# Two memory-attention layers and two gated layers on one core: a stored order for the engines, and zero matmuls in TensorE's planned waits

## The chip, the cores and the metric

The kernel runs on one core of one Trainium2 chip. The metric is the device time of that core in microseconds (us). Before the change it is 1828.59 us, the median of three runs (1826.58 to 1828.89). A change of under about 0.2% (3.7 us) can't be told from none.

The engines are named as in the profile: PE (TensorE, matmuls), PEld (its weight loads), DVE (VectorE), ACT (ScalarE), POOL (GpSimd) and SP (SyncE, which here only issues transfers).

## The reference, cut to what matters

```
def _A_ref(x, mem0, Wq, Wk, Wv, Wo, seg_len):          # x [1, 2048, 512], 32 heads of 128, seg_len 32
    mask = (idx[:, None] < 8) | (idx[:, None] >= idx[None, :])
    mem = mem0                                         # 8 rows
    for s in range(64):
        h = concatenate([mem, x[:, 32 * s:32 * s + 32]])              # 40 rows
        q, k, v = h @ Wq, h @ Wk, h @ Wv                              # per head
        p = softmax(where(mask, q @ k.T * scale, -1e9))
        o = (p @ v) @ Wo                                              # summed over heads
        mem = o[:, :8]                                 # carried to the next segment
        outs.append(o[:, 8:])

def _B_ref(x, w_gate, w_up, w_down):                   # 512 -> 1792 -> 512
    return (sigmoid(x @ w_gate) * (x @ w_up)) @ w_down

x = x + _A_ref(layernorm(x), ...)
x = x + _B_ref(layernorm(x), ...)
x = x + _A_ref(layernorm(x), ...)                      # the same weights again
x = x + _B_ref(layernorm(x), ...)
```

The 64 segments of one attention layer are a chain, for each one needs the memory rows that the segment before it made.

## The kernel before, in words

**Tiling and staging.** The four attention weights stay in SBUF. The two attention layers run side by side: layer 0 works on segment t while layer 1 works on segment t - 6, so there are 70 steps. In the middle 58 steps both layers share their matmuls, which then have 80 moving columns (40 rows of each layer); in the first 6 and the last 6 steps there is one layer and 40 columns. The lines below are those of the kernel before.

One step (`emit_step`) goes through six groups of up to six heads. For each group: Q and K (task `qk`, L734, 8 matmuls a head), a copy of the PSUM bank to `qku` on ACT, scores (`sc`, L748), mask, maximum, subtraction, exponential, sum and scaling on DVE and ACT (L762 to L779), transposes of the probabilities (`ptr`, L791), copies to `ptsb` (ACT or DVE), the product with V (`pvm`, L814), a copy to `otsb` on ACT, and the output projection (`wom`, L832), which gathers all heads in one PSUM bank. At the end of the step DVE copies the memory rows (L845, L850) into the `hT` tile of the next step, and only then can the next step's Q and K start. V of the 24 or so rows of x is made ahead in passes of 128 rows (`vmm`, L583), sent to a scratch tensor and fetched again; V of the memory rows is made in "strips" (L660).

The gated layer (`ffn`) works on blocks of 128 rows, one block of each layer for every four steps: transposes (L900, L552), gate and up (L932), tanh on ACT, the product on DVE, and the down projection (L956). Its weights don't fit and are fetched again for every block: POOL issues the transfers of `wg`, `wu` and `wd` into rings of three tiles each (L924, L925, L950).

**What sets the order.** No engine reorders whole tasks on the chip; the program's text fixes each engine's order. The kernel first records its work as 13,300 tasks with dependences (`Planner.add`), each with a modelled duration. `Planner.forward` then plays the tasks through a model of the five engines: whenever an engine is free, it takes the ready task with the greatest `tail`, if a buffer is free for it. In the kernel before, `tail` comes at first from the longest way to the end, and is then set anew 23 times by `backward`, which plays the plan in reverse; the order with the shortest modelled span is kept. The instructions are emitted in the order of the modelled start times. Every task has a latency to its reader (`LAT`, `TO_PE`, and `late` for single tasks).

Of the kernel before, what the change touches and what calls it, by code (L numbers as in the profile page):

```python
# [2 lines left out]

# [6 lines left out]
BF16 = mybir.dt.bfloat16  # L10
# [6 lines left out]
P = 128  # L17
MEM = 8
SEG = 32
L = MEM + SEG  # L20
# [11 lines left out]
def mm_ns(n):  # L32
    return max(n / 2.4 + 2.3, 26.0)

# [12 lines left out]


class Task:
    __slots__ = ("eng", "dur", "lat", "fn", "deps", "succ", "tail", "boost", "ndep", "ready", "start", "idx", "on", "fresh", "acq", "rel", "durs", "tick", "prev", "land", "adj", "banks")  # L50

    def __init__(self, eng, dur, lat, fn, boost):
        self.durs = dur if isinstance(dur, dict) else {e: dur for e in eng}
        self.eng, self.dur, self.lat, self.fn, self.boost = eng, min(self.durs.values()), lat, fn, boost
        self.deps, self.succ, self.fresh = set(), [], set()
        self.acq, self.rel = [], []
        self.on = None
        self.land = 3000.0
        self.adj = {}
        self.banks = ()  # L60


# [19 lines left out]
class Planner:  # L82
# [4 lines left out]
    TO_PE = 32.0  # L87
    WAIT = 65.0

    def __init__(self):  # L90
        self.tasks = []
        self.writer = {}
        self.readers = {}
        self.bufs = []
# [6 lines left out]
    def add(self, eng, dur, fn, r=(), w=(), lat=None, boost=0.0, use=(), late=0.0):  # L101
        engs = eng if isinstance(eng, tuple) else (eng,)
        tk = Task(engs, dur, self.LAT[engs[0]] if lat is None else lat, fn, boost)
        tk.idx = len(self.tasks)
        for k in r:
            if k in self.writer:
                tk.deps.add(self.writer[k])
                tk.fresh.add(self.writer[k])
        for k in w:
            if k in self.writer:  # L110
                tk.deps.add(self.writer[k])
            for q in self.readers.get(k, ()):
                tk.deps.add(q)
        for k in w:
            self.writer[k] = tk.idx
            self.readers[k] = []
        for k in r:
            self.readers.setdefault(k, []).append(tk.idx)
        tk.deps.discard(tk.idx)
        if late:  # L120
            tk.adj = {d: late for d in tk.fresh if self.tasks[d].eng == ("PE",)}
        self.tasks.append(tk)
        if engs[0] != "PE":
            tk.banks = tuple(k for k in r if isinstance(k, Buf) and k.pool.psum)
        for k in list(r) + list(w) + list(use):
            if isinstance(k, Buf) and (not k.users or k.users[-1] != tk.idx):
                k.users.append(tk.idx)
        return tk
# [7 lines left out]

    def plan(self, rounds=24):

        T = self.tasks
# [3 lines left out]
        for bf in self.bufs:  # L143
# [3 lines left out]
            for u in set(bf.users):  # L147
                T[u].rel.append(bf)
        for tk in reversed(T):
            m = 0.0  # L150
            for s in tk.succ:
                m = max(m, T[s].tail + self.gap(tk, T[s]))
            tk.tail = m + tk.dur + tk.boost
        best = None
        self.spans = []
        for k in range(rounds):
            if k:
                self.backward()
            order = self.forward()
            self.spans.append(self.span)  # L160
            if best is None or self.span < best[0]:
                best = (self.span, order, [tk.start for tk in order], [tk.on for tk in order], [bf.slot for bf in self.bufs])
        self.span, order, starts, ons, slots = best
        for tk, st, on in zip(order, starts, ons):
            tk.start, tk.on = st, on
        for bf, sl in zip(self.bufs, slots):
            bf.slot = sl
        return order

    def backward(self):  # L170

        T = self.tasks
        left = [len(tk.succ) for tk in T]
        rdy = [0.0] * len(T)
        free, heaps, events = {}, {}, []
        end = [tk.start + tk.dur for tk in T]
        for tk in T:
            free.setdefault(tk.on, 0.0)
            heaps.setdefault(tk.on, [])
            if left[tk.idx] == 0:  # L180
                heapq.heappush(events, (0.0, tk.idx))
        n, now = len(T), 0.0
        while n:
            while events and events[0][0] <= now:
                i = heapq.heappop(events)[1]
                if i >= 0:
                    heapq.heappush(heaps[T[i].on], (-end[i], i))
            did = False
            for e, h in heaps.items():
                if free[e] > now or not h:  # L190
                    continue
                tk = T[heapq.heappop(h)[1]]
                fin = now + tk.dur
                free[e] = fin
                tk.tail = fin + tk.boost
                heapq.heappush(events, (fin, -1))
                n -= 1
                did = True
                for d in tk.deps:
                    rdy[d] = max(rdy[d], fin + self.gap(T[d], tk))  # L200
                    left[d] -= 1
                    if left[d] == 0:
                        heapq.heappush(events, (rdy[d], d))
            if not did and n:
                now = max(now, events[0][0])

    def forward(self):
# [127 lines left out]
        return order  # L335

    def waits(self, tk, seen):

# [18 lines left out]
class Kern:  # L357
# [40 lines left out]
    def setup_tiles(self):  # L398
# [11 lines left out]
        self.ident, self.maskb, self.mask1 = cst[:, 0:P], cst[:, P:P + L], cst[0:L, P + L:P + 2 * L]  # L410
        self.negh = cst[:, P + 2 * L:P + 2 * L + 2].bitcast(F32)
        small = c.tile([P, 48], F32, name="small")
        self.lns = [small[:, 10 * i:10 * i + 10] for i in range(3)]
# [33 lines left out]
    def setup_consts(self):  # L447
# [8 lines left out]
        nc.gpsimd.affine_select(out=self.maskb[0:L, 0:SEG], in_=self.maskb[0:L, 0:SEG], pattern=[[-1, SEG]],  # L456
                                compare_op=ALU.is_ge, fill=NEG, base=0, channel_multiplier=1)
        nc.vector.memset(self.negh[:], -0.5)

    def clear(self):  # L460
# [11 lines left out]
        for k, t_ in enumerate(self.vsb):  # L472
            pl.add("POOL", 1800, lambda t_=t_: nc.gpsimd.memset(t_[32:64], 0.0),
                   w=[(n, j, k, i) for n in ("vs", "vx") for j in (0, 1) for i in (0, 1)])
# [194 lines left out]
    def emit_step(self, t):  # L669
# [11 lines left out]
        full = slice(0, LW)  # L681
        hkeys = [("hT", slot, j, k) for j in jobs for k in ("m", "x")]

        c0 = 0 if both else L * j0
# [34 lines left out]
        for g, (heads, us) in enumerate(self.groups):  # L719
# [90 lines left out]
            def pvm(us=us, ptsb=ptsb, OB=OB):  # L810
# [11 lines left out]
            pl.add("ACT", act_ns(gsz * ncol, True), lambda hs=hs, gsz=gsz, otsb=otsb, OB=OB: (  # L822
                otsb[:, hs, 0:ncol], OB[:, 0:gsz * ncol].rearrange("p (h q) -> p h q", q=ncol)), r=[OB], w=[("otsb", oi)])

# [27 lines left out]
        for idx, j in enumerate(jobs):  # L852
# [4 lines left out]
            pl.add("ACT", 160, lambda dst=dst, a=48 * j - c0: (dst, wo3(a, SEG)), r=[WB], w=[("oxT", j, oi, s % BLK)])  # L857

    def last_weights(self):

        if self.lw is None:
# [3 lines left out]
            for jp in range(self.FC // 2):  # L865
                row = []
                for nm, ring, n in (("wg", self.wg, self.NG), ("wu", self.wu, self.NG), ("wd", self.wd, self.ND)):
# [3 lines left out]
                    else:  # L871
# [6 lines left out]
                    src = self.wdv[:, 2 * jp:2 * jp + 2, :] if nm == "wd" else (self.wgv if nm == "wg" else self.wuv)[:, :, jp * 2 * P:(jp + 1) * 2 * P]  # L878
                    pl.add("POOL", 760, lambda tl=tl, src=src: nc.gpsimd.dma_start(out=tl[:, :, :], in_=src), w=keys, lat=6000.0,
                           r=[("vs", 1, (2 * (self.NSTEPS - 1) + q) % self.NV, i) for q in range(2) for i in range(2)] if k else [])  # L880
# [4 lines left out]
    def ffn(self, j, b, q0=0, nq=BLK):  # L885
# [15 lines left out]

        pl.add("PE", DC * mm_ns(P), tr, r=[("oxT", j, b % 2, q) for q in range(q0, q0 + nq)], w=[OB])
        si = self.xw[(j, b)]
# [11 lines left out]
        for jp in range(FC // 2):  # L915
# [3 lines left out]
            else:  # L919
# [3 lines left out]
                bt = ["boot"] if self.cnt["wg"] <= self.NG else []  # L923
                pl.add("POOL", 760, lambda wg=wg, fs=fs: nc.gpsimd.dma_start(out=wg[:], in_=self.wgv[:, :, fs]), r=[("wo", self.H - 1)], w=[gk] + bt, lat=6000.0)  # L924
                pl.add("POOL", 760, lambda wu=wu, fs=fs: nc.gpsimd.dma_start(out=wu[:], in_=self.wuv[:, :, fs]), r=[("wo", self.H - 1)], w=[uk] + bt, lat=6000.0)  # L925
            GB = pl.buf(self.bank, "bg")
# [16 lines left out]
        for ip in range(FC // 2):  # L943
# [3 lines left out]
            else:  # L947
                di = self.nxt("wd", self.ND)
                wd, dk = self.wd[di], ("wd", di)
                pl.add("POOL", 760, lambda wd=wd, ip=ip: nc.gpsimd.dma_start(out=wd[:], in_=self.wdv[:, 2 * ip:2 * ip + 2, :]),  # L950
                       w=[dk] + (["boot"] if self.cnt["wd"] <= self.ND else []), lat=6000.0)

# [72 lines left out]
    def run(self):  # L1025
# [4 lines left out]
        with self.tc.manual_schedule():  # L1030
            self.setup_consts()
            for tk in order:
                got = tk.fn()
                if isinstance(got, tuple) and len(got) == 3:
# [64 lines left out]
```

## Time and profile before

| | before |
|---|---|
| time, median of 3 | 1828.59 us |
| span of the profiled run | 1828.3 us |
| PE busy | 1763.5 us |
| DVE busy | 1178.3 us |
| ACT busy | 1175.2 us |
| POOL busy | 580.2 us |
| mean granted clock of PE | 0.994 |
| HBM traffic over the span | 135 GB/s |

How to read it: "busy" counts the time in which an engine has an instruction in work. A matmul's record is longer than the time until the next may start (about 200 ns against 36 ns at 80 columns), so PE can be busy through a short stall. "Idle before" is the time that an engine had nothing in work, and behind the arrow stands what ended it. The chain of waits is followed back from the last instruction. The granted clock is the share of full speed at which PE was let run.

### The profile page before, as it was taken

Reading aid. Unit: us, or ns where it says so; the run is one execution under the profiler, and the core shown is the slowest. Engines: PE = TensorE matmul, PEld = TensorE weight load, DVE = VectorE, ACT = ScalarE, POOL = GpSimd, SP = SyncE. Lnnn points to the kernel's source line nnn. Section 1 sums busy time; section 2 is a strip of 40 time slices with the busy share of each in tenths; the row PEclk is TensorE's granted clock in tenths of the full one; section 3 lists DMA queues with packets and bytes.
Section 4 is the critical chain, followed back from the end, with each engine's and each line's share of the span. In section 5 each row is a group of like instructions: output and inputs, shape, how many; then the busy total and the mean of one; then the engine's idle time right before and its main releaser. Section 6 shows DMA issues by size and latency. Waiting matters only on the chain.

```text
span 1828.3 us, 91963 instructions
## 1 busy us (share of the span) xinstructions
PE 1763.5 (96%) x39743; PEld 1522.8 (83%) x39942; DVE 1178.3 (64%) x3933; ACT 1175.2 (64%) x2969; POOL 580.2 (32%) x838
## 2 busy tenths in 40 slices
PE   7999999999999999999999999999999999999998
PEld 3677787988888898988888888888888898888786
DVE  4466565676666666666666667666766667556665
ACT  5665666676666666665666666666666666566564
POOL 7223031413333242313333142323324241333322
PEclk9989999999999999999999999999999999999999
DMA  9734252636455364635446364545546453554543
GB/s 344 237 108 140 55 150 81 196 103 175 143 158 159 113 181 123 173 115 170 145 137 177 112 190 117 153 139 151 163 123 191 117 165 105 155 148 123 166 126 107
DMA packets 137096, 271.18 MB, mean 148 GB/s; under 512 B 32698, under 2 KB 69186, under 8 KB 136690
## 3 DMA queue, kind: packets, MB, share of 16 engines
q0 software_dynamic: 56736, 183.35, 34.1%
q1 hardware_dynamic: 79954, 81.94, 15.5%
q8 instruction: 313, 5.13, 1.2%
q14 instruction: 93, 0.76, 0.1%
HBM read 220.93 MB, written 26.21 MB: 135 GB/s over the span
## 4 chain that ended last, share of the span: by engine, by line
PE 85%; ACT 5%; DVE 3%; SPq 3%; issue 2%; DMA 1%; POOL 0%; ACTq 0%; POOLq 0%; DVEq 0%
PE bank L734 31%; PE bank L832 17%; PE bank L932 9%; PE bank L660 7%; PE bank L583 6%; PE bank L956 4%; PE bank L748 4%; PE bank L814 3%; SPq L484 3%; PE bank L791 2%; ACT qku L1039 1%; ACT ptsb L1039 1%; ACT otsb L1039 1%; DVE st L762 1%; PE bank L552 1%
## 5 line engine op out<-in xcount | busy, mean ns | idle before, releaser
L734 PE MATMUL bank<-hT,wq_sb 128*128 128x80 bf16 (+1 forms) x8960 | 622.3, 198 | 9.0 <-issue 5.0
L734 PE MATMUL bank<-hT,wk_sb 128*128 128x80 bf16 (+1 forms) x8960 | 621.5, 198 | 2.8 <-DMA wk_sb<-in_A_Wk_dram 2.5
L1039 ACT CAST qku<-bank 128x480 bf16<-128x480 f32 (+3 forms) x770 | 391.4, 512 | 254.8 <-PE bank L734 182.8
L734 PEld LDWEIGHTS <-wq_sb 128*128 128x128 bf16 x8960 | 454.8, 99 | 37.7 <-issue 27.5
L734 PEld LDWEIGHTS <-wk_sb 128*128 128x128 bf16 x8960 | 450.5, 99 | 5.0 <-DMA wk_sb<-in_A_Wk_dram 3.0
L762 DVE TENSOR_TENSOR st<-bank,cst 40x240 f32<-40x240 f32 (+3 forms) x768 | 279.5, 368 | 225.0 <-PE bank L748 216.0
L832 PE MATMUL bank<-otsb,wo_sb 128*128 128x80 bf16 (+1 forms) x8960 | 366.8, 198 | 10.8 <-ACT otsb L1039 9.1
L924 POOL DMA_DIRECT2D wg<-in_B_w_gate_dram x217 | 164.9, 760 | 650.3 <-PE bank L932 626.6
L832 PEld LDWEIGHTS <-wo_sb 128*128 128x128 bf16 x8960 | 341.8, 99 | 24.0 <-issue 15.1
L1039 ACT CAST otsb<-bank 128x480 bf16<-128x480 f32 (+3 forms) x420 | 196.2, 486 | 72.8 <-PE bank L814 55.1
L950 POOL DMA_DIRECT2D wd<-in_B_w_down_dram x217 | 153.5, 710 | 155.7 <-PE bank L791 71.8
L1039 ACT COPY ptsb<-bank 40x240 bf16<-40x240 bf16 (+2 forms) x552 | 173.9, 316 | 40.5 <-PE bank L791 32.2
L772 ACT ACTIVATE st<-st 80x240 f32<-80x240 f32 (+3 forms) x420 | 159.4, 382 | 37.3 <-DVE st L769 33.1
L774 DVE TENSOR_REDUCE small<-st 80x6 f32<-80x240 f32 (+3 forms) x420 | 151.8, 364 | 46.6 <-ACT st L772 43.6
L932 PE MATMUL bank<-xnT,wg 128*128 128x128 bf16 (+2 forms) x1784 | 172.1, 218 | 3.6 <-issue 2.5
L932 PE MATMUL bank<-xnT,wu 128*128 128x128 bf16 (+2 forms) x1784 | 171.2, 218 | 0.0
L925 POOL DMA_DIRECT2D wu<-in_B_w_up_dram x217 | 162.8, 750 | 3.2 <-issue 2.5
L769 DVE TENSOR_TENSOR st<-st,small 80x240 f32<-80x240 f32 (+3 forms) x420 | 154.1, 369 | 4.0
L767 DVE TENSOR_REDUCE small<-st 80x6 f32<-80x240 f32 (+3 forms) x420 | 152.7, 365 | 5.5
L748 PE MATMUL bank<-qku 128*128 128x80 bf16 (+1 forms) x2240 | 154.3, 198 | 1.6 <-issue 0.5
L779 DVE TENSOR_TENSOR pb<-st,small 80x240 bf16<-80x240 f32 (+3 forms) x420 | 152.7, 369 | 4.5
L542 POOL TENSOR_TENSOR small<-small,cst 128x1 f32<-128x1 f32 (+1 forms) x80 | 44.4, 557 | 348.3 <-DVE small L541 345.3
(93 smaller groups left out, 2252.8 us busy)
## 6 DMA issues: line engine op xcount, KB each, us to landing
wg<-in_B_w_gate_dram POOLq DMA_DIRECT2D x220, 256.0 KB, 4.1
wu<-in_B_w_up_dram POOLq DMA_DIRECT2D x220, 256.0 KB, 4.8
wd<-in_B_w_down_dram POOLq DMA_DIRECT2D x220, 256.0 KB, 4.8
vsb<-scr SPq DMA_DIRECT2D x476, 48.0 KB
vsb<-sst SPq DMA_DIRECT2D x480, 32.0 KB
scr<-vst SPq DMA_DIRECT2D x120, 96.0 KB
wq_sb<-in_A_Wq_dram SPq DMA_DIRECT2D x10, 384.0 KB
wk_sb<-in_A_Wk_dram SPq DMA_DIRECT2D x10, 384.0 KB
```

Of the source, the lines that this page charges most:

```text
L734: nc.tensor.matmul(o_ap, lhsT=W[:, c, h * P:(h + 1) * P], rhs=mv(c), start=(c == 0), stop=(c == DC - 1))
L748: nc.tensor.matmul(s_all(SB)[:, w0 + i, :], lhsT=fview(qku[:, i, 0, 0:1], [(1, P)]), rhs=qku[:, i, 1, 0:ncol], start=True, stop=True)
L762: pl.add("DVE", dve_ns(n, True), lambda gsz=gsz, hs=hs, st=st, SB=SB, pj_=pj_, npj_=npj_, mk=mk, idx=idx: nc.vector.tensor_tensor(out=st[p ...
L767: pl.add("DVE", dve_ns(n), lambda hs=hs, st=st, mx=mx: nc.vector.tensor_reduce(out=mx[pr, hs], in_=st[pr, hs], axis=AX.X, op=ALU.max), r=s ...
L769: pl.add("DVE", dve_ns(n), lambda gsz=gsz, hs=hs, st=st, mx=mx: nc.vector.tensor_tensor(out=st[pr, hs], in0=st[pr, hs], in1=mx[pr, hs].uns ...
L772: pl.add("ACT", act_ns(n), lambda hs=hs, st=st: nc.scalar.activation(out=st[pr, hs], in_=st[pr, hs], func=ACTF.Exp, scale=self.scale), r=s ...
L832: nc.tensor.matmul(WB[:, c * ncol:(c + 1) * ncol], lhsT=self.wo[:, h, c * P:(c + 1) * P], rhs=otsb[:, hl, 0:ncol], start=(h == 0 and c == ...
L924: pl.add("POOL", 760, lambda wg=wg, fs=fs: nc.gpsimd.dma_start(out=wg[:], in_=self.wgv[:, :, fs]), r=[("wo", self.H - 1)], w=[gk] + bt, la ...
L925: pl.add("POOL", 760, lambda wu=wu, fs=fs: nc.gpsimd.dma_start(out=wu[:], in_=self.wuv[:, :, fs]), r=[("wo", self.H - 1)], w=[uk] + bt, la ...
L932: nc.tensor.matmul(gu[:, 2 * i + k, 0:n], lhsT=W[:, c, i * P:(i + 1) * P], rhs=xnT[:, c, rw], start=(c == 0), stop=(c == DC - 1))
L950: pl.add("POOL", 760, lambda wd=wd, ip=ip: nc.gpsimd.dma_start(out=wd[:], in_=self.wdv[:, 2 * ip:2 * ip + 2, :]), w=[dk] + (["boot"] if se ...
L1039: nc.scalar.copy(out=dst, in_=src)
```

## The change

The search for an order at build time is taken out. In its place the source holds a string, `SEQUENCE`, from which each of the 13,300 tasks gets its rank; `forward` is run once with these ranks in place of the tails. The string was found ahead of time by local search over the plan model, whose durations and latencies are corrected at the same time: the issue cost of a matmul, the memset of `vsb`, the landing of the gated layer's weights, the copy to `otsb` and the transposes of L900.

Besides, `warm` walks over PE's planned tasks. Where the plan has a wait of over 250 ns ahead of a task that takes a fresh PSUM bank, and the window of 3413 ns around it would be filled to under 0.6 (or it is in the first 8 us), matmuls of a tile of zeros (`hot`) are put into the wait. They write the bank that the task then overwrites, and are sized to end 120 ns before the planned wait does.

The lines L525 to L1041 of before stand some 90 lines further down in the changed kernel. The diff, without the string:

```
-    return max(n / 2.4 + 2.3, 26.0)
+    return max(n / 2.4 + 2.5, 25.0)
...
+SEQUENCE = r"""
...
+    SPAN, COLD, WARM0 = 3413.0, 8000.0, 1200.0
...
-        for tk in reversed(T):
-            m = 0.0
-            for s in tk.succ:
-                m = max(m, T[s].tail + self.gap(tk, T[s]))
-            tk.tail = m + tk.dur + tk.boost
-        best = None
-        self.spans = []
-        for k in range(rounds):
-            if k:
-                self.backward()
-            order = self.forward()
...
+        code = lzma.decompress(base64.b85decode("".join(SEQUENCE.split())), ...)
+        left = list(range(len(T)))
+        for k, (q,) in enumerate(struct.iter_unpack("<H", code)):
+            T[left.pop(q)].tail = -float(k)
+        order = self.forward()
...
+    def warm(self, order):
...
+            gap, on = tk.start - end, [bf for bf in tk.acq if bf.pool.psum]
+            if gap > 250.0 and on:
+                cold = tk.start < self.COLD
...
+                if cold or lo < 0.6 * self.SPAN:
+                    n = int((gap - 120.0) * (1.2 if cold else 2.4)) // P
+                    if n > 0:
+                        fill[tk.idx] = (on[0], n)
...
+        nc.vector.memset(self.hot[:], 0.0)
...
-            pl.add("POOL", 1800, lambda t_=t_: nc.gpsimd.memset(t_[32:64], 0.0),
+            pl.add("POOL", 560, lambda t_=t_: nc.gpsimd.memset(t_[32:64], 0.0),
...
-                otsb[:, hs, 0:ncol], OB[:, 0:gsz * ncol].rearrange("p (h q) -> p h q", q=ncol)), r=[OB], w=[("otsb", oi)])
+                otsb[:, hs, 0:ncol], OB[:, 0:gsz * ncol].rearrange("p (h q) -> p h q", q=ncol)), r=[OB], w=[("otsb", oi)], late=55.0)
...
-        pl.add("PE", DC * mm_ns(P), tr, r=[("oxT", j, b % 2, q) for q in range(q0, q0 + nq)], w=[OB])
+        pl.add("PE", DC * mm_ns(P) + 94.0, tr, r=[("oxT", j, b % 2, q) for q in range(q0, q0 + nq)], w=[OB])
...
-                pl.add("POOL", 760, lambda wg=wg, fs=fs: nc.gpsimd.dma_start(out=wg[:], in_=self.wgv[:, :, fs]), r=[("wo", self.H - 1)], w=[gk] + bt, lat=6000.0)
+                pl.add("POOL", 760, lambda wg=wg, fs=fs: nc.gpsimd.dma_start(out=wg[:], in_=self.wgv[:, :, fs]), r=[("wo", self.H - 1)], w=[gk] + bt, lat=5200.0)
...
+            fill = self.pl.warm(order)
             for tk in order:
+                if tk.idx in fill:
+                    B, n = fill[tk.idx]
+                    while n > 0:
+                        m = min(n, 4)
+                        nc.tensor.matmul(B[:, 0:m * P], lhsT=self.hot[:], rhs=fview(self.hot[:, 0:1], [(0, m), (1, P)]), start=True, stop=True)
+                        n -= m
                 got = tk.fn()
```

The latency of 6000 becomes 5200 in the same way for `wu`, `wd` and the last block's weights.

## The prediction

> **What bounds the kernel now.** I read the page's busy shares first, then the chain that ended last, then what TensorE (PE) waited for, then stretches of time with the granted clock, and last single stretches of the chain and the timeline.
>
> ```profile
> PE 1763.5 (96%) x39743; PEld 1522.8 (83%) x39942; DVE 1178.3 (64%) x3933; ACT 1175.2 (64%) x2969; POOL 580.2 (32%) x838
> PE 85%; ACT 5%; DVE 3%; SPq 3%; issue 2%; DMA 1%; POOL 0%; ACTq 0%; POOLq 0%; DVEq 0%
> ```
>
> PE holds the chain and no other engine is near it. Busy counts the pipeline's latency (about 200 ns a matmul), so it hides short stalls. The chain shows what a matmul costs in a stream:
>
> ```profile
> 649.34 1.84 PE bank L660 x32
> ...
> 654.09 0.89 PE bank L932 x16
> ...
> 657.13 3.44 PE bank L734 x96
> ```
>
> ```profile
> 116.20 2.56 PE bank L734 x96
> ```
>
> 3.44/96 = 35.8 ns at 80 columns, 2.56/96 = 26.7 ns at 40 (25 ns in a pure stream), 0.89/16 = 56 ns at 128, 1.84 us for 32 strip matmuls; the long down-projections issue every 216 ns. With the counts of the groups kept apart by shape: 27,296 matmuls of 80 columns x 35.8 = 977 us; 4,992 of 40 x 25 = 125; 3,908 of 128 x 56 = 219; 72 strip tasks x 1.84 = 132; 1,198 of 512 x 216 = 259 (the instruction order has all of them, the trace lacks 199); small ones 8. Sum 1720 us. The span is 1828.3, so 108 us are not issue: 7.6 us before the first and after the last matmul, some 13 us of half clock, and about 87 us of gaps. Summed from the trace's matmul start times, the gaps are 20 us before 200 us, 50 us from 200 to 1700, 15 us after.
>
> ```profile
> PE bank L832 <- ACT otsb L1039: 9.1, 31, 1.0
> PE bank L552 <- DVE xn L543: 6.9, 5, 3.3
> PE bank L734 <- issue: 5.2, 6, 2.2
> PE bank L525 <- DMA hff<-in_A_mem_dram: 4.1, 1, 4.1
> ```
>
> The dearest wait is that of the output projection (L832) for ACT's copy of the PV result. This view counts only the part after the pipeline has drained; in start times the stalls before L832 are 18.7 us in the middle stretch alone.
>
> ```profile
> 0.00:14.90 14.90, 5.40 (x24) 2.44 (x24) 9.26 (x28) 3.33 (x8) 13.02 (x30) 1.00 0.87 297
> 14.90:60.00 45.10, 43.85 (x441) 23.75 (x447) 19.82 (x62) 30.14 (x60) 26.20 (x52) 1.00 1.08 370
> 127.55:141.20 13.65, 11.88 (x200) 8.70 (x200) 7.21 (x29) 5.99 (x21) 1.09 (x2) 0.50 0.19 54
> 200.00:1700.00 1500.00, 1469.82 (x32875) 1295.12 (x33044) 986.26 (x3272) 980.48 (x2407) 468.64 (x652) 1.00 0.50 144
> 1728.40:1731.80 3.40, 3.40 (x63) 2.25 (x63) 1.05 (x5) 1.39 (x5) 0.00 (x0) 0.50 0.02 5
> 1806.90:1810.30 3.40, 3.27 (x46) 2.73 (x47) 0.50 (x2) 1.58 (x6) 0.00 (x0) 0.50 0.02 5
> ```
>
> ```profile
> 10.98 3.57 PE L583 MATMUL bank<-wv_sb,xvf 128*128 128x512 bf16 x8 [0.62 <-DVE xvf L1041]
> ...
> 15.63 8.58 PE L583 MATMUL bank<-wv_sb,xvf 128*128 128x512 bf16 x38
> ```
>
> Columns of the six stretches: stretch, length, busy of PE, PEld, DVE, ACT, POOL, clock, DMA share, GB/s. The clock is 0.50 in one stretch of 13.65 us and two of 3.4 us. The first row's 1.00 misleads, for the clock's record begins at 14.9 us: eight 512-column matmuls take 3.57 us there (446 ns each), 38 take 8.58 us just after (226 ns). The start is at half clock too. The transfers fill the DMA engines until 60 us (0.87, then 1.08).
>
> **What the Trainium skill says.** "TensorE: Matmul & The Clock Gate", Part 1, says that PE's clock halves after a window of about 3.4 us with too little activity and returns after a busy window. This trace agrees: two dips last 3.4 us, the long one four windows. Part 2 of that page, on the steps of a matmul, says that matmuls stay in program order, only weight loads are pulled ahead; so one matmul that waits holds all behind it, as the table of waits shows. Its section "Back-to-back issue gap" gives N/2.4 + 2.5 ns for N columns: 55.8 ns at 128, 215.8 at 512; the trace has 56 and 216. No section says whether matmuls of zeros count as activity, and no row of this trace shows one. Part 4 says that transposes hardly count, so instructions do differ.
>
> **The change part by part.**
>
> *Zero matmuls (28 places, 243 units of 128 columns).* In the changed instruction order 99 units stand ahead of the first transposes and V passes, 104 in the single-layer steps near the start (places that had the half clock), 40 in those near the end. Waits hide them if the planned waits are real. The worst case is that none of the 144 later units is hidden: 144 x 56 ns = 8 us; the best is 0. I take 0.5 us, for each fill is sized 120 ns short of its wait. The first 15 matmuls need only a memset; at half clock they take 59 x 107 ns = 6.3 us and end before the first transposes' data (7.68 us in the timeline). What they can win: the matmuls issued before 14.9 us have 2.5 us of issue time at full speed, so 2.5 us; I take 1.5, since the weights' transfers then set part of the pace. In the long dip 6.5 us of issue are lost; part of that stretch waits anyway (11.88 busy of 13.65), so I take 5. The later dips and the end lose 3.9; I take 2, since the tail is a chain from engine to engine. If zeros do not count, all three are 0, as low bound. Together -8.5 + 0.5 = -8 us.
>
> *The order.* Task counts stay (4,213 on PE, one copy moves between ACT and DVE), so the issue floor stays at 1720 us. What moves is how much PE work stands between a producer and its consumer. I measured this distance in issue time for every handover in both orders, and from the trace of before the mean gap at each distance. For PV to output projection: 365 ns where under 500 ns stands between, 212 up to 700, 129 up to 850, then 3 to 36. In the middle stretch before has 22, 10 and 10 such places; the changed order has 6, 3 and 7. The sums over all distances, before to changed: PV to L832 (output projection) 16.1 to 9.2 us; memory copy to the next step's Q/K (L734) 4.0 to 1.6; Q/K copy to scores (L748) 1.9 to 1.1; probability copies to PV (L814) 5.4 to 7.7, worse. Sum 27.4 to 19.6: -7.8 us. In the single-layer ends the sums stand still (17.4 to 17.5).
>
> The other 23 us of gaps in the middle (transposes, strips, masks, queues on ACT and DVE) the count of distances doesn't see. I let them shrink in the same share, 28%: -6.5 us. Low bound 0; high bound half of them, 11.
>
> *Durations and latencies of the model* (mm_ns, memset 560 in place of 1800, weights' landing 5200 in place of 6000, 55 ns on the PV copy, 94 ns on the transposes) cost no instruction; they act through the order and the fills. One has a price: weight tiles are refilled later. Of 655 refills, 27 had under 7.5 us of PE work between last read and next use, now 100; under 7 us 2, now 24. The transfer lands 4.2 us after issue in the median and 7.8 at most, plus up to 1.5 us for two issues on POOL (749 ns each). Queued behind a late weight are all of PE's matmuls. Between nothing and 24 x 0.5 = 12 us; I take 0.5 us, for at 7 us the median has 1 us to spare.
>
> Sum: -8 - 7.8 - 6.5 + 0.5 = -21.8, from 1828.6 to 1806.8, rounded 1806.
>
> **The rivals.** (1) *Clock only.* The distances shrank by too little, or ACT and DVE arrive late in the new order and the gap moves from L832 to L814 (its sum rose). For it: 50 us of gaps in the middle, of which only 27 lie at counted handovers. Then 1828.6 - 8 = 1820. (2) *Half of all gaps go.* For it: a search can trade waits of all engines at once, and the shortest distances fell from 42 places to 16. Against it: ends that stand still, and stalls of up to 2.2 us "issue" that no order touches. Middle 50 to 25 and ends 35 to 27 give -33, with the clock -41: 1788. (3) *Slower.* The order is fitted to modelled times; late weights (+12), unhidden zeros (+8) and zeros that don't warm the clock (0 for -8.5), with the waits moved and not removed, give 1828.6 + 20 = 1848 at worst, 1838 with half. For it: 100 tight refills. Against it: the 27 tight refills of before show no PE wait on wg or wd at all.
>
> **How the numbers follow.** Forecast 0.55, clock only 0.17, half of the gaps 0.18, slower 0.10. Predicted: 1806. The range reaches to 1780, under rival 2, and to 1826, over rival 1; outside lie the worse part of rival 3 and a tenth at the low side. Within 0.2% (3.7 us) fall 0.02 of rival 1 and 0.02 of rival 3: faster 0.88, same 0.04, slower 0.08.
>
> **What would show it.** Right: the clock in the 20 us around 130 us is 0.95 or more (0.69 before), eight 512-column matmuls near 11 us take 1.8 us and not 3.57; the wait of L832 for otsb falls from 31 times and 9.1 us to below 20 times; the gaps from 200 to 1700 us fall from 50 us to about 36. Wrong: the dips stay (zeros don't count); a row of PE waiting for DMA wg, wu or wd; PE's waits at L814 growing by as much as those at L832 fall; gaps that stay at 50 us.

## The result, and the profile after

| | before | after |
|---|---|---|
| median of 4 runs each | 1828.13 us | 1822.29 us |
| range | 1826.58 to 1828.89 | 1819.79 to 1825.01 |
| ratio after/before | | 0.9969, 95% interval 0.9951 to 0.9988 |

The change is faster, by 5.8 us. The forecast was 1806 us, 22 us faster. A second session with the changed kernel, `after_again`, gave 0.9968 (0.9956 to 0.9980).

Page of the changed kernel, busy shares and the chain by engine:

```profile
PE 1782.4 (98%) x40014; PEld 1524.2 (84%) x40014; DVE 1152.5 (63%) x3935; ACT 1184.0 (65%) x2968; POOL 581.1 (32%) x837
...
PE 85%; DVE 5%; SPq 3%; ACT 2%; issue 2%; DMA 2%; POOL 1%; ACTq 0%; DVEq 0%; POOLq 0%
```

PE has 72 matmuls that are new, the zeros (two expectations below say 87; the trace has 72, of 243 units of 128 columns), which issue for about 16 us, 8 of them in the first 19 us. PE still holds 85% of the chain, so a busier PE says nothing here. What it waited for (line, what came last, us in total, times, longest):

```profile
PE bank L638 <- POOL small L628: 5.9, 1, 5.9
PE bank L821 <- issue: 5.9, 5, 1.8
PE bank L901 <- DMA vsb<-sst: 3.8, 3, 1.8
...
PE bank L901 <- ACT ptsb L1135: 2.1, 10, 0.3
PE bank L919 <- ACT otsb L1135: 1.8, 7, 0.4
...
PE bank L1021 <- DMA wg<-in_B_w_gate_dram: 0.4, 1, 0.4
```

L919 is the output projection (L832 before). Its wait for ACT's copy has gone from 31 times and 9.1 us to 7 times and 1.8 us. L901 is the product with V (L814 before, 2.7 us for ptsb) and now also waits for a transfer. L638 (L552 before) is new at the top: one wait of 5.9 us for POOL, at the start.

Stretches of the changed kernel, with the columns of the six stretches before:

```profile
14.90:60.00 45.10, 42.69 (x396) 22.42 (x395) 20.05 (x63) 27.66 (x57) 23.81 (x43) 1.00 0.97 323
120.00:140.00 20.00, 16.77 (x503) 13.83 (x500) 13.32 (x48) 10.69 (x36) 8.29 (x12) 1.00 0.58 166
200.00:1700.00 1500.00, 1488.65 (x33251) 1301.49 (x33248) 969.83 (x3312) 996.98 (x2423) 471.70 (x655) 1.00 0.51 145
```

The clock around 130 us is 1.00 (0.69 before), but from 14.9 to 60 us PE issued 396 matmuls, some of them zeros, where it had issued 441, and the transfers fell from 370 to 323 GB/s. In the middle it issued 33,251 for 32,875 (the trace of before lacks some records, so this is only a direction).

Where the time went is seen best by progress: from the start times of the matmuls I took the moment at which so many of PE's 1720 us of issue work, zeros not counted, were done.

| issue work done | before | after | after less before | gained in between | forecast |
|---|---|---|---|---|---|
| 60 us | 76.8 | 83.5 | +6.7 | +6.7 (start) | -1.5 |
| 190 us | 228.7 | 234.7 | +5.9 | -0.8 (single-layer steps) | -5 |
| 1600 us | 1699.9 | 1696.6 | -3.3 | -9.2 (middle) | -14.3 |
| end | 1824.4 | 1818.1 | -6.3 | -3.0 (end) | -2 |

So the gain was there, and 6.7 us of it were given back in the first 84 us. `after_again` repeats it: +6.9, +4.4, -7.0, -9.0 at the four marks.

### The profile page after: what moved, and what is told of

Its sections match the earlier page's. It is cut to its first block, busy times and chain, and to the rows that moved or that the text cites. A ratio compares the mean times of both kernels' runs of the same rounds, so it can differ in the third digit from the quotient of the medians.

```text
span 1822.5 us, 92040 instructions
## 1 busy us (share of the span) xinstructions
PE 1782.4 (98%) x40014; PEld 1524.2 (84%) x40014; DVE 1152.5 (63%) x3935; ACT 1184.0 (65%) x2968; POOL 581.1 (32%) x837
## 3 DMA queue, kind: packets, MB, share of 16 engines
q1 hardware_dynamic: 80066, 82.14, 16.1%
## 4 chain that ended last, share of the span: by engine, by line
PE 85%; DVE 5%; SPq 3%; ACT 2%; issue 2%; DMA 2%; POOL 1%; ACTq 0%; DVEq 0%; POOLq 0%
PE bank L821 30%; PE bank L919 16%; PE bank L1021 10%; PE bank L746 7%; PE bank L669 6%; PE bank L1045 5%; PE bank L901 4%; PE bank L835 4%; SPq L570 2%; PE bank L878 2%; DVE st L849 1%; ACT ptsb L1135 1%; DMA vsb<-sst 1%; DVE small L854 1%; PE bank L638 1%
## 5 line engine op out<-in xcount | busy, mean ns | idle before, releaser
L919 PE MATMUL bank<-otsb,wo_sb 128*128 128x80 bf16 (+1 forms) x8960 | 365.2, 198 | 4.3 <-ACT otsb L1135 1.8
L919 PEld LDWEIGHTS <-wo_sb 128*128 128x128 bf16 x8960 | 339.0, 99 | 21.5 <-issue 6.7
L1135 ACT COPY ptsb<-bank 40x240 bf16<-40x240 bf16 (+3 forms) x535 | 170.1, 320 | 49.3 <-PE bank L878 39.0
L628 POOL TENSOR_TENSOR small<-small,cst 128x1 f32<-128x1 f32 (+1 forms) x80 | 45.0, 563 | 408.4 <-DVE small L627 400.4
L835 PE MATMUL bank<-qku 128*128 128x80 bf16 (+1 forms) x2240 | 162.8, 198 | 1.3 <-issue 0.7
```

The lines of the kernel that those rows point to most:

```text
L835: nc.tensor.matmul(s_all(SB)[:, w0 + i, :], lhsT=fview(qku[:, i, 0, 0:1], [(1, P)]), rhs=qku[:, i, 1, 0:ncol], start=True, stop=True)
L919: nc.tensor.matmul(WB[:, c * ncol:(c + 1) * ncol], lhsT=self.wo[:, h, c * P:(c + 1) * P], rhs=otsb[:, hl, 0:ncol], start=(h == 0 and c == ...
L1135: nc.scalar.copy(out=dst, in_=src)
```

## The experiments

Each ratio is to the kernel before in the same session (its medians lie from 1825.87 to 1828.13). The last four columns are the marks of the table above, less those of before's profile. That profile is of one execution 3 to 4 us above before's later medians, so the marks compare kernels with each other better than with before. Nor do the profiles of one order agree fully: between the 190 and the 1600 mark six profiles with before's order stand from +0.9 to -4.9 (mean -2.6; before, e3, e9, e10, e12, e13) and eight with the stored order from -9.2 to -13.9 (mean -11.7; after, after_again, e1, e2, e5, e6, e8, e11). The order is worth about 9 us there.

| run | median us | ratio | 95% interval | 60 | 190 | 1600 | end |
|---|---|---|---|---|---|---|---|
| after_again | 1821.32 | 0.9968 | 0.9956-0.9980 | +6.9 | +4.4 | -7.0 | -9.0 |
| e1_no_zeros | 1818.63 | 0.9962 | 0.9948-0.9976 | +6.3 | +3.3 | -9.8 | -12.9 |
| e2_memset_late | 1818.80 | 0.9964 | 0.9950-0.9978 | +7.5 | +5.3 | -8.4 | -11.5 |
| e3_before_zeros | 1820.44 | 0.9971 | 0.9961-0.9980 | -0.4 | -1.7 | -6.5 | -8.0 |
| e4_list_order | 1842.78 | 1.0093 | 1.0079-1.0108 | +2.6 | +1.4 | +15.4 | +14.5 |
| e5_write_later | 1817.70 | 0.9943 | 0.9928-0.9958 | +1.8 | +1.5 | -8.8 | -13.3 |
| e6_start_both | 1817.28 | 0.9943 | 0.9932-0.9955 | +2.1 | +0.1 | -13.8 | -17.5 |
| e7_spread_late | 1835.86 | 1.0056 | 1.0044-1.0068 | +7.5 | +7.2 | +9.5 | +5.4 |
| e8_start_no_zeros | 1815.42 | 0.9940 | 0.9928-0.9952 | +1.6 | -0.6 | -10.7 | -13.8 |
| e9_zeros_not_at_start | 1820.81 | 0.9973 | 0.9961-0.9985 | -0.4 | -2.1 | -6.3 | -9.2 |
| e10_tile_alone | 1826.31 | 0.9999 | 0.9989-1.0009 | 0.0 | +0.4 | +1.3 | -0.8 |
| e11_x_first | 1816.44 | 0.9939 | 0.9926-0.9951 | +0.5 | 0.0 | -12.2 | -14.7 |
| e12_short_zeros_81 | 1825.30 | 0.9988 | 0.9981-0.9996 | 0.0 | +0.3 | -4.6 | -4.1 |
| e13_short_zeros_30 | 1825.50 | 0.9991 | 0.9981-1.0001 | +1.4 | +0.5 | -2.3 | -4.9 |

### Zeros and order apart

`e1_no_zeros` is the changed kernel without the zeros, `e3_before_zeros` the kernel before with `warm` and its zeros (81 matmuls, sized by its own plan), `e4_list_order` the changed kernel with corrected model and zeros, but with before's search of 24 rounds in place of the stored string.

```
e1:  -            fill = self.pl.warm(order)
     +            fill = {}
e3:  before, with `rate`, `warm`, `hot` and the loop over `fill` of the change
e4:  -SEQUENCE = r"""
     +    def plan(self, rounds=24):      # plan and backward as before
```

> The changed kernel itself once more, as the mark for the runs beside it: 4 to 8 us under the kernel before, by every theory.

> The changed kernel without its 87 zero matmuls, the stored order and all real work as in the changed kernel. If the zeros buy the clock as forecast: half clock returns for some 13 us in all in the single-layer steps near 130 us and near the end, and at the start to about 15 us, and the time is 4 to 8 us longer than the changed kernel's 1822, near 1828. If those steps are bound by the chain from engine to engine and not by PE's rate, the dips return but the time stays within 2 us of 1822. If the zeros cost more than they hide, it is faster, below 1820.

> The kernel before with the zero matmuls alone, in the waits that its own plan shows; order, model and work as before. If the zeros buy the clock: no half clock near 130 us, and the time is 3 to 8 us under 1828, near 1822 to 1825, which would be all that the change brought. If the single-layer steps are bound by the chain from engine to engine: the dips go but the time stays within 2 us of 1828.

> The changed kernel (its corrected model and its zeros) with the search of before (24 rounds of forward and backward) in place of the stored sequence. If the stored sequence is what shortened the gaps between 200 and 1700 us, those gaps are near 45 to 50 us again here, and the time is 5 to 12 us over the changed kernel's, 1827 to 1834, less what its start does better. If the corrected model or the zeros did it, the time is within 2 us of 1822.

Zeros alone on before's order give 0.9971, and the stored order alone gives 0.9962. Together they give no more than either: 0.9968 and 0.9969, with intervals that overlap all of these. The new model and its zeros with a list search are no gain at all: 1.0093, with all of the loss in the middle (+1.4 to +15.4 between the marks). So the string is worth about 20 us against a list search under its own model, but only about 6 us against before's list order. Which of the model's new numbers spoils the list search was not tried apart. Row of PE's waits in `e4_list_order`:

```profile
PE bank L869 <- ACT otsb L1085: 8.3, 37, 0.5
```

The 37 waits for otsb are back there.

What the zeros did to the clock is seen in the same stretch of four kernels. The kernel before:

```profile
120.00:140.00 20.00, 16.69 (x395) 13.67 (x391) 13.15 (x49) 10.58 (x37) 5.87 (x10) 0.69 0.50 145
```

before with zeros (`e3_before_zeros`):

```profile
120.00:140.00 20.00, 17.20 (x419) 13.46 (x408) 13.00 (x49) 11.02 (x38) 5.72 (x10) 0.83 0.49 143
```

the changed kernel without them (`e1_no_zeros`); with them it is the row with 1.00 above:

```profile
120.00:140.00 20.00, 16.89 (x495) 14.79 (x492) 13.56 (x49) 11.86 (x41) 8.20 (x12) 0.84 0.57 163
```

These rows alone don't show that zeros count as activity. Dips differ from run to run: on before's order the one near 130 us lasts 13.7 us in before, 10.2 in `e10_tile_alone`, and 6.8 in `e12_short_zeros_81` and `e13_short_zeros_30`, which have no zeros there, as in `e3_before_zeros`, which has them. Three other figures do show it.

- At the start of the changed kernel PE has nothing but zeros. The first eight are issued about 427 ns apart, and from 4.75 us on they are 216 ns apart. In the eight profiles with wide zeros in the first microseconds the clock is first full at 4.2 to 6.9 us, in the eight without at 13.2 to 17.7 us; 30 or 81 zeros of 8 columns did not warm it.
- On before's order, by the mean granted clock of each run, half clock takes 16.4 us in 18 runs of before and 5.5 us in six runs of `e9_zeros_not_at_start`.
- In the stored order the dip near 130 us lasts 10.2 us in each of the three profiles without zeros, and none to 3.4 us in the five with them.

The Trainium skill, "TensorE: Matmul & The Clock Gate", Part 1, calls the window free-running and its phase different from run to run; the changed kernel's two profiles, without that dip in one and with 3.4 us of it in the other, agree.

What half clock costs can be read from the runs of one kernel, which differ by chance. In the 35 runs of before in the last session it takes 11 to 26 us, and with each microsecond more of it the time is about 0.3 us longer (correlation 0.5); in the 22 runs of `e12_short_zeros_81` it is 0.4 (0.9). Matmuls that wait for nothing would give 0.5.

In the stored order no gain is seen: from the 60 mark to the 190 mark after gains 0.8 us, `after_again` 2.5, and `e1_no_zeros`, with its long dip, 3.0. In those steps only one layer is at work, and matmuls may wait for a chain through DVE and ACT that a faster PE doesn't shorten; that is argued, not shown. A rival stands in the traces: from 60 to 200 us PE waited 5.2 us in after and 2.7 in `after_again` for no task but, as the last part of the experiments shows, for its own instructions, and 2.2 us in `e1_no_zeros`.

### The start

In the stored order PE's first work starts late. PE in the changed kernel:

```profile
1.00 5.16 PE L1127 MATMUL bank<-hot 128*128 128x512 bf16 x15 [1.00 <-DVE cst L544]
12.05 0.61 PE L638 MATMUL bank<-cst,xn 128*128 128x128 bf16 x4 [5.89 <-POOL small L628]
```

and POOL:

```profile
2.60 3.54 POOL L559 MEMSET vsb<- 32x2048 bf16 x2
...
6.49 1.80 POOL L559 MEMSET vsb<- 32x2048 bf16 x1
...
10.92 1.10 POOL L628 TENSOR_TENSOR small<-small,cst 128x1 f32<-128x1 f32 x2
```

The layer norm's power on POOL (L628) stands behind three memsets of 1.80 us; "PSUM — Partial Sum Buffer" in the Trainium skill, section "Engine vs sequencer instructions", says that POOL's queue is strictly first in, first out, and so it looks. The model's 560 ns is wrong there: the plan has the first transposes at 7.6 us and they came at 12.05. The zeros were sized for the short wait, PE stood still for 5.9 us behind them, and the clock's record shows half clock again from 11.5 to 14.9 us. (The kernel before booked 1800 ns for this memset.) `e2_memset_late` puts the memsets behind the first two powers.

```
+        n = [k for k, tk in enumerate(order) if tk in self.pw][1]
+        order = [tk for tk in order[:n + 1] if tk not in self.vz] + self.vz + [tk for tk in order[n + 1:] if tk not in self.vz]
```

> The changed kernel with the three memsets of vsb moved on POOL behind the first two inverse square roots (L628); nothing else moves, all work is done. The trace of the changed kernel has these memsets at 1.80 us each where the model has 560 ns, and PE waited 5.9 us for the inverse square root behind them. If that delay is what the start lost: the first transposes come near 8 us and not at 12.05, the wait of SyncE for the first scratch write shrinks by about 4 us, and the time falls by 4 to 7 us, to 1815 to 1818. If the transfers of the weights set the start's pace anyway, PE starts earlier but the time stays within 1.5 us of 1822.

The first work came 3.6 us sooner, and nothing of it was left at the 60 mark (+7.5). So POOL isn't what holds the start; something later is. SyncE's waits in the first 80 us, and its timeline, in the changed kernel:

```profile
SPq L1131 <- ACT wg L1135: 10.6, 1, 10.6
SPq L570 <- DMA wv_sb<-in_A_Wv_dram: 2.2, 1, 2.2
```

```profile
16.41 0.94 SPq L570 DMA_DIRECT2D wq_sb<-in_A_Wq_dram  x2
...
27.99 0.33 SPq L1131 DMA_DIRECT2D scr<-wg  x1
28.36 0.46 SPq L570 DMA_DIRECT2D wq_sb<-in_A_Wq_dram  x1
```

After two Q weight transfers at 16.41 us SyncE came at 17.35 to a write to the scratch tensor, whose bytes ACT had not yet copied, and waited there until 27.99. All other attention weights stood behind it. The DMA engines' share and rate from 10 to 80 us, in slices of 1.75 us:

```profile
DMA  9999999853588999999999999999999999999974
GB/s 394 401 370 373 377 348 342 288 176 105 155 160 254 295 308 395 365 382 394 398 388 390 363 363 336 332 365 377 359 359 383 377 379 364 337 289 329 309 234 156
```

From 24 to 29 us they ran half empty, and the rate is back only at 36 us, in a stretch where before kept them full (to 60 us). The kernel before, from 20 to 30 us:

```profile
20.00:30.00 10.00, 9.89 (x75) 4.60 (x76) 3.14 (x10) 6.29 (x11) 7.14 (x14) 1.00 1.08 370
```

The plan did not see it: it books a weight transfer on SyncE by its bytes (at 300 GB/s, 3.5 us for 1 MB), so in the plan SyncE comes to the write at 23.17 us, when the copy (done at 22.92) is there. On the chip SyncE handed these transfers over in 0.4 to 0.5 us each and came 5.8 us sooner, while the copy came 5 us later. `e5_write_later` moves that one write six transfers down; `e6_start_both` adds the later memsets to it; `e8_start_no_zeros` takes the zeros out as well; `e11_x_first` moves the first part of the V weights behind the first three loads of x.

```
e5:  +        sp = [tk for tk in order if tk.on == "SP"]
     +        k = next(i for i, tk in enumerate(sp) if tk.eng == ("SP", "POOL"))
     +        tk, to = sp[k], sp[k + 6]
     +        order.remove(tk)
     +        order.insert(order.index(to) + 1, tk)
e6:  e5 and e2
e8:  e6, and    fill = {}
e11: e8, and    order.remove(sp[0])
                order.insert(order.index(sp[3]) + 1, sp[0])
```

> The changed kernel with one transfer moved: the first scratch write on SyncE (scr from wg) stands six weight transfers later in SyncE's order; all work is done. In the changed kernel SyncE waited 10.6 us for the copy that this write sends, with the weights queued behind it, and the DMA engines fell from 370 to as low as 105 GB/s between 24 and 36 us. If this wait is what the start lost (6.7 us behind the kernel before when 60 us of PE work are done): the hole in the transfers goes, PE is 4 to 6 us earlier at that mark, and the time is 3 to 6 us under the changed kernel's. If the start is behind because of its late first transposes or the order of its V passes, the hole goes and the time stays within 1.5 us.

> The changed kernel with both edits of the start: the scratch write six weight transfers later on SyncE, and the three vsb memsets behind the first two inverse square roots on POOL; all work is done. If SyncE's wait alone set the start: the same as with the write moved alone, within 1.5 us. If both delays add: 1.5 to 4 us under that one. If neither counts: within 1.5 us of the changed kernel.

> The changed kernel with both edits of the start (scratch write later, vsb memsets later) and without the 87 zero matmuls; all real work is done. Beside the same kernel with its zeros (0.9943 of before): if the zeros are worth nothing in the stored order, it is within 0.15% of that, 0.993 to 0.996; if they buy half of what they were forecast to, it is 0.9965 or more; if they cost what they issue (13 us, partly unhidden), it is under 0.992.

> The changed kernel without zeros, with both edits of the start, and with the first part of the V weights behind the first three loads of x on SyncE (it stood ahead of them); all real work is done. If the 2 us that the start still loses against the kernel before come from x standing behind weights: the first transposes come 1 us earlier or more, PE is within 1 us of the kernel before when 60 us of its work are done, and the time is 1 to 3 us under the same kernel without this edit (0.9940 of before). If they come from the order of the V passes: within 1 us of it.

The stretch from 20 to 30 us in the changed kernel:

```profile
20.00:30.00 10.00, 10.00 (x54) 4.76 (x52) 6.14 (x21) 6.43 (x12) 7.38 (x14) 1.00 0.72 220
```

and in `e5_write_later`, with SyncE's wait at that write:

```profile
20.00:30.00 10.00, 10.00 (x54) 4.78 (x53) 5.71 (x19) 6.45 (x11) 7.53 (x15) 1.00 1.08 356
```

```profile
SPq L1136 <- ACT wg L1140: 3.7, 2, 3.1
```

356 GB/s for 220; the 60 mark falls from +6.9 to +1.8 and the time from 0.9968 to 0.9943, 4.6 us of 1827. `e6_start_both`, `e8_start_no_zeros` and `e11_x_first`, all with the write moved, lie at 0.9943, 0.9940 and 0.9939. Four kernels show it: one transfer in the wrong place cost nearly as much as the whole change gained. The memsets are worth nothing in time with the write moved either. Loading x first takes the 60 mark to +0.5, but the time doesn't follow. `e8_start_no_zeros` and `e11_x_first` beat both kernels, by 11 us and, by the ratios, by about 5.

### The middle: where the waits went

A clean ledger needs a trace of before's order with all its records: that is `e3_before_zeros`. Summed from start times between 200 and 1700 us, with the time that the matmuls themselves take to issue removed:

| what PE stood before or within, us | before's order (e3) | stored order (after) |
|---|---|---|
| output projection | 16.1 | 4.1 |
| product with V | 7.4 | 18.6 |
| strips | 6.7 | 5.8 |
| scores | 3.5 | 1.0 |
| down projection | 3.2 | 0.6 |
| Q and K | 2.1 | 1.0 |
| transposes, V passes, gate and up | 3.3 | 7.5 |
| sum | 42.4 | 38.6 |

Before's own profile sums to 46.8 (it lacks records, so its split by task isn't used), `e1_no_zeros` to 35.3. The sums fall by less than the 9 us between the marks' means, for after is the slowest of its order's eight profiles in the middle and e3 nearly the fastest of its six. The order took 12.0 us away from the output projection, and the product with V took 11.2 of them back. How it did is seen in one place of the changed kernel. PE:

```profile
898.74 0.27 PE L835 MATMUL bank<-qku 128*128 128x80 bf16 x3
899.03 0.44 PE L901 MATMUL bank<-ptsb,vsb 104*128 104x80 bf16 x6
899.77 0.38 PE L901 MATMUL bank<-ptsb,vsb 104*128 104x80 bf16 x6 [0.30 <-ACT ptsb L1135]
```

ACT at the same time:

```profile
897.82 0.35 ACT L1135 COPY ptsb<-bank 40x240 bf16<-40x240 bf16 x1
898.19 0.41 ACT L859 ACTIVATE st<-st 80x240 f32<-80x240 f32 x1
898.62 1.09 ACT L1135 COPY ptsb<-bank 40x240 bf16<-40x240 bf16 x3
```

Three copies run back to back on ACT until 899.71, and the second product starts 0.06 us later. The task's two copies wait in one engine's queue, one behind the other. Of the 86 places where PE stood still before a product with V, 81 end within 150 ns of the last ptsb copy, and in 75 of these both copies were on one engine. That they share an engine doesn't set the two orders apart, though: both copies are on one engine for 306 of the 348 products of the middle here and for 285 of 348 in `e3_before_zeros`. The room on PE shrank too: at under 850 ns of PE work between transposes and product there are 29 places here and 3 in e3, and they cost about 4 and 1 us. And the distance on PE no longer tells the wait: with 850 to 950 ns of PE work between transposes and product, 48 places cost 1.6 us in before and 49 cost 5.1 in after. The rest, 3.9 us, are fetches of V that had not landed:

```profile
1521.75 0.35 PE L901 MATMUL bank<-ptsb,vsb 104*128 104x80 bf16 x5 [1.77 <-DMA vsb<-sst]
```

`e7_spread_late` was to make the scheduler leave more room there: the copy to ptsb gets 100 ns more latency, with the ranks unchanged.

```
-                pl.add(("ACT", "DVE"), copy_ns(nu * nj * L, True), spread, r=[PB], w=[("ptsb", pi, i)])
+                pl.add(("ACT", "DVE"), copy_ns(nu * nj * L, True), spread, r=[PB], w=[("ptsb", pi, i)], late=100.0)
```

> The changed kernel with 100 ns more latency in the model between the transposes of the probabilities and the copies to ptsb (late=100 on the task spread), the stored ranks as they are: forward then lets PE do other work that much longer ahead of PV. If PV's waits (18 us in the middle stretch against 8 us before the change) come from a handover that the model has too short: they fall to 8 to 12 us and the time is 4 to 9 us under the changed kernel's. If they come from ACT and DVE being late by their own queues, the waits stay or move to the output projection, and the time is within 2 us. Against it stands that the ranks were searched for the old latency; if they are worth nothing away from it, the time is over 1830.

It is slower, 1.0056, and the waits for otsb return:

```profile
PE bank L919 <- ACT otsb L1135: 5.8, 17, 0.6
```

One latency in the model moves every later choice, and here the stored ranks lost their gain with it. So this run doesn't settle what room before the product with V is worth; that a shorter ACT queue there would bring the 11 us is argued from the trace and was not tried alone.

### What zeros give to before's order

> The kernel before with zero matmuls only after the first 8 us of its plan (the single-layer steps and the end), none ahead of the first transposes; order and work as before. With all its zeros it was 0.9971 of before. If the later zeros carried that, it stays at 0.9965 to 0.998; if the zeros at the start did, it is 0.999 or more.

> The kernel before with the tile of zeros and its memset but no zero matmul: order, model and work as before. It shifts the tiles behind it in SBUF and nothing else. If the zeros made the 5 us that the kernel before gained with them, this is within 0.1% of before, 0.999 to 1.001. If the shift of the tiles or chance did, it is 0.998 or less.

> The kernel before with 81 zero matmuls of 8 columns, all ahead of the first PE task, where PE waits for 4 us anyway; nothing else. They warm nothing later, but all later PE instructions stand as much further down as with the 81 zeros of the run that gained 5 us. If the place of the instructions closes the gaps without a wait (6 to 7 us between 200 and 1700 us before): those gaps fall under 2 us and the time is 0.9965 to 0.9985 of before. If the warm clock made the 5 us: 0.9995 to 1.001, gaps at 5 us or more.

> The same with 30 short zeros. If the place of the instructions matters, the gaps without a wait and the time may land anywhere from 0.996 to 1.001 and differ from the run with 81. If it doesn't, both are within 0.1% of before.

```
e9:  e3, and  fill = {tk.idx: fill[tk.idx] for tk in order if tk.idx in fill and tk.start > 8000.0}
e10: e3, and  fill = {}
e12: e10, and ahead of PE's first task
     +                    for _ in range(81):
     +                        nc.tensor.matmul(tk.acq[0][:, 0:8], lhsT=self.hot[:], rhs=self.hot[:, 0:8], start=True, stop=True)
e13: the same with 30
```

The tile and its memset alone do nothing (0.9999). The zeros of the start are not needed (0.9973 without them, 0.9971 with). So about 5 us come from the 69 later matmuls. Of these, 1.3 to 1.7 us lie in the single-layer steps by the marks. The 1.5 to 2.9 us at the end are not clearly theirs, for `e10_tile_alone` and `e13_short_zeros_30` gain 2.1 and 2.6 us there without them.

The middle has next to no zeros (8 between 200 and 1600 us), and yet its mark moves by more, through gaps of 0.4 to 2.2 us ahead of PE instructions that wait for nothing: 3 of them, 3.8 us, in before's profile, 4 and 4.7 us in `e10_tile_alone`, none in `e3_before_zeros`, one of 0.6 us in `e9_zeros_not_at_start`. Short zeros of 8 columns at the start, which warm nothing later but shift PE's instructions, leave none (81) or 2 of 1.3 us (30), and gain 0.1% with intervals that end at 0.9996 and 1.0001. So the shift is worth about 2 us (at most 3.5 by the interval), and some 3 us are left for the clock. That fits the price of half clock above: 11 us less of it at 0.3 us each.

The traces tell what PE waits for in these gaps: its own instructions. One of them, near the end of before, and the queue that carries the core's program, from before's page:

```profile
1807.03 0.42 PE L932 MATMUL bank<-xnT,wg 128*128 128x96 bf16 x3 [1.93 <-issue]
```

```profile
q8 instruction: 313, 5.13, 1.2%
```

A packet of 16 KB began on that queue 2.6 us before PE went on. So it is with nearly all of them. From 60 us on, the 16 profiles hold 98 waits of PE of over 0.35 us that the view names "issue", for it shows nothing that PE waited for; at 94 of these the last packet of q8 had begun 2.2 to 3.0 us before PE went on, where a random moment falls so in 14% of cases. There is one packet for every 255 of PE's 79,884 matmuls and weight loads, which fits that the places change when matmuls are added. The waits come to 3.4 to 11.6 us a profile, mostly in the single-layer steps and at the end; in 12 of the 16 that is more than this change gained. They are no artefact of the recording, for they stand in profiles with all matmul records too (after, `e5_write_later`, `e13_short_zeros_30`). What earlier fetches would save was not tried.

## Why the prediction was right and wrong

**Right: the side, and the order's first effect.** Faster, as forecast, and within the range. L832's wait for otsb was to fall below 20 times; it fell to 7. The clock around 130 us was to be at least 0.95; it is 1.00, though 0.91 in `after_again`. The gaps from 200 to 1700 us were to fall from 50 to about 36 us; by the ledger they fell from 46.8 to 38.6. Weights fetched later were to cost 0.5 us; PE waited for `wg` once, 0.4 us. The zeros hide in their waits: nothing in the marks speaks against the 0.5 us put down for them.

**Wrong: the start.** The step that failed is "What they can win: ... I take 1.5" together with "In the single-layer ends the sums stand still". It measured the order by PE's distances alone. The start is set by SyncE's queue and the DMA engines, as the prediction had read from the six stretches itself, and the changed order on SyncE was never looked at. In place of -1.5 the runs show +6.7, of which moving one scratch write takes back 5 (`e5_write_later`); loading x first takes another 1 at the mark. The zeros could win nothing there, for PE's first real work came 4.4 us later than planned and the clock had dropped again. The sign of eight 512-column matmuls in 1.8 us near 11 us could not come in after; in `e2_memset_late` they took 1.90 us at 11.54. (In before they are 427 ns apart from start to start; the 446 of the prediction counts the end of the last one.)

**Mis-sized: the long dip.** Forecast -5, measured -0.8 in after and -2.5 in `after_again`, and 1.3 to 1.7 on before's order. That zeros count and shorten the dip was right. The price, 5 us for a dip of 13.65, is 0.37 us a microsecond, and the runs of before show about 0.3. But the dip of that one profile was taken for what every run loses: its half clock comes to 23 us, the mean of the runs is 17. And in the stored order the shorter dip brought nothing that the marks show; whether the chain through other engines or the fetch of PE's instructions took it stays open.

**Mis-sized: the middle.** Forecast -14.3, measured -9.2 (-11.4 in `after_again`), about -9 between all the profiles of the two orders. The terms PV to L832, memory copy to Q and K, and Q/K copy to scores fell as said or further. The term "probability copies to PV" was put at 5.4 to 7.7 and is 7.4 to 18.6 on the chip: the mean gap at each distance, taken from before's trace, does not carry over (1.6 and 5.1 us at the same distance), and the stored order has more places with little room. How far ACT's queue makes this is argued, not shown. The 6.5 us put down for uncounted gaps were a guess in the same share; strips, masks and transposes did not shrink together.

**The later dips and the end.** -2 forecast, -3.0 measured: right by luck, for the forecast put it down to zeros, and `e1_no_zeros` gains 3.1 us there without any.

**The rivals.** The first, the gap moving from L832 to L814, is what happened in the middle, and its 1820 lies nearest, by luck: its clock gain of 8 us didn't come, and an order gain of 9 us was in good part eaten by the start. "Half of all gaps" did not occur. The slower rival named late weights; a late transfer it was, but on SyncE at the start and not on POOL in the middle.

## What to carry to other kernels

When a scheduler or a stored order moves work, compare the order on every queue, those that only issue transfers first: an in-order queue that meets an early wait holds everything behind it, and a plan that books the transfer's time on the issuing engine can't see this. Look at what stands ahead of the producer on the producer's engine, not only at the distance on PE. Half clock is not worth half its length: here it was 0.3 to 0.4 us a microsecond. Compare waits with the packets of the instruction queue before calling them unexplained. One profile of before is not a yardstick for differences of a few microseconds.

## What the runs showed of the hardware

- Matmuls of a tile of zeros bring the clock up: with nothing else on PE they went from 427 to 216 ns each at 4.75 us (after). On before's order they cut half clock from 16.4 to 5.5 us a run (`e9_zeros_not_at_start`). Yet on the stored order they are worth nothing that five runs can tell (0.9943 with, 0.9940 without, the write moved in both).
- A microsecond of half clock went with 0.3 us of time in 35 runs of before and 0.4 in 22 runs of `e12_short_zeros_81`.
- A memset of 32x2048 bf16 takes POOL 1.80 us; the source had been changed from 1800 to 560 ns for it.
- PE waits for its own instructions: 3.4 to 11.6 us a profile in waits of 0.4 to 3.3 us, and at 94 of 98 the last packet of the instruction queue had begun 2.2 to 3.0 us before PE went on. The places change when PE instructions are added.
